# A feed-forward matrix as seven block products for eight, with its activations through DRAM

## The chip, the cores and the metric

The kernel is one program on one core of a Trainium2 chip. Its engines work side by side, each through its own list in order, and wait for each other by semaphores: TensorE (PE: matmuls; PEld: its weight loads), VectorE (DVE), ScalarE (ACT), GpSimd (POOL) and SyncE (SP), which issues nearly all DMAs. The metric is the device time of one execution in microseconds (us). Before the change it is 814.73 us, the median of three runs (813.27 to 820.41).

## The reference

One transformer block over 2048 positions of width 512: a normalised, modulated input goes through memory-augmented attention (32 heads of 16, four segments of 512 positions) and an output projection; the result is normalised again and goes through a feed-forward part of width 1792 with a GELU.

```python
h = _layernorm(x) * (1 + ca) + sa
x = x + ga * _A_ref(h, A_wq, A_wk, A_wv, A_wo, A_beta)   # attention, then o @ wo
h = _layernorm(x) * (1 + cb) + sb
x = x + gb * (_gelu(h @ w1 + b1) @ w2 + b2)
```

All is in float32. On TensorE the kernel writes each float32 factor as a high part (its cast to fp32r) and a low part (the rest), and a product as three matmuls: high by high, low by high, high by low.

## The kernel before, in words

Three stages follow each other, with overlaps. The first makes q, k, v and the memory terms. The second is attention: 64 steps, each for two heads of one segment, in an order that tables of numbers (`PRM`) write out by hand. A position in these tables is ten times the step plus a place in it. A step computes scores (L609) and their masked row maxima on VectorE (L616), the scores again transposed (L698) with exponentials on ScalarE (L713, L724), the causal masks on GpSimd (L701), and PV products (L738).

Four heads' PV output goes to DRAM and comes back regrouped; a *group* is eight heads of one segment, 16 in all, numbered U. VectorE takes the reciprocal of its row sums (L773), which goes to DRAM (`RD`) and is loaded back broadcast (`rbB`); the group is multiplied by it and the memory term is added (L787, L789; the *mix*), then it is cast and split (`oh`, `ol`). The memory term itself is first multiplied by a broadcast `rm` on GpSimd (L794). Groups 13 to 15 are mixed on VectorE, earlier ones on GpSimd. Four groups and the split `wo` make a segment's output projection: 48 matmuls (L815) in four blocks of positions `b`. Segments 0 to 2 do this during attention, in the one PSUM bank `mm`; segment 3 after it. The residual is added (L833) and the rows go to DRAM as `X2D`.

The third stage is the feed-forward part. A segment's rows are normalised (`ln2_*`), turned by four transposes for each of four blocks `d` of the width (L162), modulated on ScalarE and split. Segment 0's turns stand in attention, the other segments' in the feed-forward part. The first matrix has 14 output blocks of 128. For one block and one segment `ffn1_mm` issues 12 matmuls (four blocks `k` by three, L989) into one of three banks; ScalarE's GELU reads the bank (L992); VectorE casts and subtracts (L140, L141). All stays in SBUF. Four blocks later `ffn2` uses the result in 12 matmuls for the second matrix (L1073), into four banks `acc`. So the two matrices alternate: 12 matmuls of the first, 12 of the second, 56 times. The split weights of both stay in SBUF after the first segment.

Between attention and this alternation stands a transition: four blocks of the first matrix and the first half of segment 3's projection occupy TensorE while groups 14 and 15 come back from DRAM.

## Time and profile before

| | |
|---|---|
| median of three runs | 814.73 us (813.27 to 820.41) |
| the profiled execution, first to last instruction | 811.6 us |
| TensorE busy in it | 796.0 us |
| attention's last PV product ends at | 484.6 us |
| from there to the end | 327.0 us |
| matmuls 128x512 of the first / second feed-forward matrix | 672 / 672 |

The profiled execution's own time is its span; what lies around it in a run is part of the median's 3.1 us more. In a list of groups a line shows its place in the code, the engine, what is written from what, the count, the time busy, the mean of one in ns, and the engine's idle time before it with what ended that. In a list by time a line begins with the start and the duration in us; a bracket at its end names the wait before it. In a table of stretches each engine stands with its busy time and, in brackets, its instructions.

### The profile page before, as it was taken

The numbers are of one execution on the slowest core, as the hardware profiler recorded it, in microseconds if no ns is written. First come the engines' busy times: TensorE is split into PE (matmuls) and PEld (weight loads), VectorE is DVE, ScalarE is ACT, GpSimd is POOL, SyncE is SP. The second block draws the span as 40 slices with busy tenths as digits, with TensorE's granted clock in tenths as the row PEclk, the third lists the DMA queues.
The fourth block names the chain that finished last, engine by engine and source line by source line (L and its number), as shares of the span: only waits on it lengthen the run. The fifth ranks groups of instructions, "written<-read, shape, count | busy, mean of one in ns | idle before, by whom it ended". The sixth has DMA issues, their size and how long they took to land.

```text
span 811.6 us, 13638 instructions
## 1 busy us (share of the span) xinstructions
PE 796.0 (98%) x4669; PEld 546.9 (67%) x4669; DVE 502.7 (62%) x1373; ACT 368.5 (45%) x734; POOL 287.3 (35%) x508
## 2 busy tenths in 40 slices
PE   8999999999999999999999999999999999999998
PEld 4877777866444455445544548788888888888887
DVE  6686696469878877896687627874542353324223
...
GB/s 339 183 311 253 271 181 218 159 353 129 171 171 182 165 208 175 238 199 181 177 183 206 172 192 192 213 120 101 25 79 1 52 67 38 1 1 104 1 1 52
DMA packets 83566, 123.03 MB, mean 152 GB/s; under 512 B 14116, under 2 KB 46244, under 8 KB 82984
## 3 DMA queue, kind: packets, MB, share of 16 engines
...
q8 instruction: 36, 0.59, 0.3%
...
HBM read 75.60 MB, written 46.15 MB: 150 GB/s over the span
## 4 chain that ended last, share of the span: by engine, by line
PE 75%; DMA 8%; ACT 5%; DVE 4%; POOL 4%; issue 3%; SPq 1%; ACTq 0%; DVEq 0%; POOLq 0%
PE acc L1073 18%; PE f1b L989 16%; PE pv L738 6%; PE att L698 5%; PE q L330 5%; PE att L609 5%; PE k L330 4%; PE mm L815 3%; PE v L481 3%; DMA RD<-dn 2%; DMA rbB<-RD 2%; ACT pt L713 1%; PE nu L453 1%; DMA qst<-ms 1%; POOL pt L701 1%
## 5 line engine op out<-in xcount | busy, mean ns | idle before, releaser
L616 DVE CUSTOM_DVE_ANT_0 dump<-att,maskb 128x512 bf16<-128x512 f32 (+2 forms) x384 | 192.2, 553 | 27.2 <-PE att L609 24.3
L992 ACT ACTIVATE gt<-f1b,b1t 128x512 f32<-128x512 f32 x56 | 38.5, 688 | 245.8 <-PE f1b L989 195.0
L713 ACT ACTIVATE pt<-att 128x512 f32<-128x512 f32 (+1 forms) x256 | 126.1, 557 | 44.6 <-PE att L698 44.3
L701 POOL TENSOR_SCALAR_AFFINE_SELECT pt<-pt 128x256 f32<-128x256 f32 x256 | 100.1, 408 | 80.1 <-ACT pt L713 50.1
L140 DVE CAST gh<-gt 128x512 fp32r<-128x512 f32 x56 | 23.8, 425 | 163.0 <-ACT gt L992 163.0
L698 PE MATMUL att<-qst,kst 99*128 99x512 bf16 (+3 forms) x512 | 106.6, 300 | 5.5 <-ACT pt L724 2.1
L609 PE MATMUL att<-kst,qst 96*128 96x512 bf16 (+2 forms) x384 | 94.2, 326 | 0.7 <-DVE nm L616 0.2
L738 PE MATMUL pv<-pt,V 128*32 128x512 f32 (+2 forms) x992 | 88.3, 442 | 0.1
L1073 PE MATMUL acc<-w2h,gh 128*128 128x512 f32 (+1 forms) x224 | 86.7, 387 | 0.0
L1073 PE MATMUL acc<-w2l,gh 128*128 128x512 f32 (+1 forms) x224 | 86.0, 384 | 0.4 <-DVE w2l L141 0.4
L1073 PE MATMUL acc<-w2h,gl 128*128 128x512 f32 (+1 forms) x224 | 85.9, 383 | 0.0
L698 PEld LDWEIGHTS <-kst 99*128 99x128 bf16 x512 | 42.9, 97 | 56.9 <-issue 39.7
L989 PE MATMUL f1b<-hodd,w1h 128*128 128x512 f32 x224 | 73.7, 390 | 0.0
L724 ACT ACTIVATE pt<-att 128x512 f32<-128x512 f32 (+1 forms) x128 | 57.1, 512 | 22.9 <-PE att L609 19.9
L153 POOL TENSOR_SCALAR crs<-cmv 128x4 f32<-128x4 f32 x4 | 1.0, 247 | 170.8 <-DVE cmv L150 170.7
L609 PEld LDWEIGHTS <-qst 96*128 96x128 bf16 x384 | 33.2, 98 | 39.9 <-issue 24.6
L1073 PEld LDWEIGHTS acc<-w2l,gh 128*128 128x128 f32 x224 | 42.0, 188 | 9.1 <-DVE w2l L141 0.9
L989 PEld LDWEIGHTS f1b<-hodd,w1h 128*128 128x128 f32 x224 | 42.1, 188 | 8.6
L1073 PEld LDWEIGHTS acc<-w2h,gl 128*128 128x128 f32 x224 | 42.1, 188 | 8.4
L1073 PEld LDWEIGHTS acc<-w2h,gh 128*128 128x128 f32 x224 | 42.1, 188 | 8.3
L738 PEld LDWEIGHTS pv<-pt,V 128*32 128x32 f32 x992 | 22.2, 108 | 36.8 <-issue 26.2
L989 PE MATMUL f1b<-C0hh,w1l 128*128 128x512 f32 x112 | 43.7, 390 | 0.2 <-DVE w1l L141 0.2
...
## 6 DMA issues: line engine op xcount, KB each, us to landing
...
```

The costliest lines, as they stand in the source:

```text
L330: pe.matmul(ps, a[:, k, 128 * g:128 * g + 128], b[k], start=(k == 0 and i == 0), stop=(k == KB - 1 and i == 2))
L481: pe.matmul(ps, a[k][:, 128 * b:128 * b + 128], w[:, k, :], start=(k == 0 and i == 0), stop=(k == KB - 1 and i == 2))
L609: pe.matmul(ps, q_of(P, h, i), k_of(P, h, 128 * (i + 1)), start=True, stop=True)
L616: v.tensor_tensor_reduce(out=dump[n_dump[0] % 2][:, :n], in0=src, in1=maskb[:, 512 - n:], scale=-1.0, scalar=-4 * NEG, op0=ALU.add, op1=AL ...
L698: pe.matmul(ps, k[:99, e, 128 * j:128 * j + 128], q[:99, e, 128 * j:512], start=True, stop=True)
L701: pool.affine_select(out=t, in_=t, pattern=pattern, compare_op=ALU.is_ge, fill=0.0, base=0, channel_multiplier=-1)
L713: act.activation(pt[:, h, :], ps[:, :n], AF.Exp, scale=0.25)
L724: act.activation(pt, pv_, AF.Exp, scale=0.25)
L738: pe.matmul(ps[32 * c:32 * c + 32, lo:hi], V[4 * s + j][:, VW * hd:VW * hd + 32], pt[:, c % 2, lo - o:hi - o], start=start, stop=stop)
L989: pe.matmul(ps, a[:, k, :], b[k], start=(i == 0), stop=(i == 11))
L992: act.activation(g, ps, AF.Gelu_apprx_tanh, bias=b1t[:, f:f + 1])
L1073: pe.matmul((mm if lo else acc[b])[:, lo:hi], a[:, c], w[:, lo:hi], start=(f == 0 and i == 0), stop=(last and i == 2))
```

## The change

The first matrix is computed for two segments at once. Take output blocks f and f + 7 of the matrix, two segments a and b, and the two halves of the width over which the sum runs: a two-by-two product of blocks. Eight block products make it; Winograd's form of Strassen's method makes it from seven, with sums and differences of the blocks ahead and behind. Each block product here is six matmuls (two `k` by three). Seven of them are called a *quad*: 14 quads, seven for segments 0 and 1, seven for 2 and 3.

- Differences of the activations (`r_sub`, four times two operations on 128x512 for each pair of segments) and of the weights (`w_sub`, four operations on 128x256 for each quad) are made on GpSimd, then split: the high part on ScalarE, the low part on VectorE.
- In a quad ScalarE copies the bank X three times while products are still added to it, VectorE adds three times, and four GELUs follow. Their results go to DRAM (`GD`).
- The second matrix starts after the last quad. It loads the activations back from `GD`, three steps ahead, and splits them (`split_g`). It uses eight banks in turn by segment. Its weights are loaded, scaled on GpSimd and split during the last seven quads, into SBUF that the first pair's activations leave.
- Segment 1 is normalised and turned in attention as segment 0 is. Segment 2's output projection moves behind attention, ahead of segment 3's.

```diff
- 'wo': [[2, 10, 10, 10], [6, 10, 11, 11], [2, 10, 10, 11]],
+ 'wo': [[2, 10, 10, 10], [6, 10, 11, 11]],
- 'ht': 481,
- 'htd': 20,
- 'ln': [312, 339, 374, 408],
+ 'ht': [[465, 474, 481, 494], [614, 622, 629, 636]],
+ 'ln': [[312, 339, 374, 408], [498, 522, 566, 574]],
- 'wout': ['vvvv', 'vava', 'vava'],
+ 'wout': ['vvvv', 'vava', 'vvvv'],
- 'w1at': [58, 59, 60],
+ 'w1at': [58, 60],
...
+        def r_sub(p, n):
+            x, y = {"t1": ("b12", "b11"), "t2": ("b22", "b11"), "t3": ("b22", "b12"), "t4": ("b21", "b22")}[n]
+            for o, i, j in zip(hk(p, RAW[n]), hk(p, x), hk(p, y)):
+                pool.tensor_tensor(out=o, in0=i, in1=j, op=ALU.subtract)
...
+        def r_lo(p, n, k):
+            src = hk(p, RAW.get(n, n))[k]
+            v.tensor_tensor(out=R[p][n][1][k], in0=src, in1=R[p][n][0][k].bitcast(F32), op=ALU.subtract)
...
+            pool.tensor_tensor(out=b[:, i], in0=x, in1=y, op=ALU.add if i == 0 else ALU.subtract)
...
+        def prod(n, name, ps, start):
+            t, i = PW[name]
+            wh, wl = wt1[t][n % 2]
+            rh, rl = R[n // FH][name]
+            for k in range(2):
+                for c, (a, b) in enumerate(((wh, rh), (wl, rh), (wh, rl))):
+                    pe.matmul(ps, a[:, i, k, :], b[k], start=start and k == 0 and c == 0, stop=k == 1 and c == 2,
+                              skip_group_check=not start)
...
+            if not last:
+                prod(n, "b11", X, True)
+                act.activation(s1, X, AF.Copy)
+                step(0)
+                prod(n, "b21", Y, True)
+                add(s1, Y)
+                g_out(n, s1, s1, 0, 0)
+                step(1)
+            if not first:
+                prod(n - 1, "t4", bx[(n - 1) % 2], False)
+                g_out(n - 1, bx[(n - 1) % 2], s4, 1, 0)
+            step(2)
+            if not last:
+                prod(n, "t2", X, False)
+                act.activation(s2, X, AF.Copy)
+            step(3)
+            if not first:
+                o = st["2"][(n - 1) % 2]
+                prod(n - 1, "b22", bv[(n - 1) % 2], False)
+                add(o, bv[(n - 1) % 2])
+                g_out(n - 1, o, o, 0, 1)
+            step(4)
...
+            prod(n, "t1", V_, True)
+            step(5)
+            prod(n, "t3", X, False)
+            act.activation(s3, X, AF.Copy)
+            add(s3, V_)
+            g_out(n, s3, s3, 1, 1)
+            step(6)
...
+        for m in range(4):
+            bg(2 * FH - 1, 6, load_g, m)
+        for m in range(2):
+            bg(2 * FH, 2 + m, split_g, m)
...
+        for n, i, f, m in ((2, 3, r_split, "b11"), (3, 2, r_split, "b21"), (4, 0, r_sub, "t1"), (4, 1, r_split, "b22"),
+                           (4, 2, r_sub, "t3"), (4, 4, r_split, "t1"), (5, 0, r_sub, "t2"), (5, 1, r_split, "t3"),
+                           (5, 4, r_split, "t2"), (5, 5, r_sub, "t4"), (6, 1, r_split, "t4")):
+            bg(n, i, f, 1, m)
```

A *step* here is a place after a product, to which `bg` hangs other work: splits, sums and loads for later quads.

Three places of the instruction lists are spoken of below. The first is TensorE's list where attention ends; the first row is the last of the PV products. Before:

```order
L738 MATMUL att_2009<-pt_2_5897,V_153 32x256 x2
L989 MATMUL f1b_5946<-C0hh_0_4974,w1h_5987 128x512
L989 MATMUL f1b_5946<-C0hh_0_4974,w1l_5988 128x512
L989 MATMUL f1b_5946<-C0hl_0_4975,w1h_5987 128x512
L989 MATMUL f1b_5946<-C0hh_1_5095,w1h_5987 128x512
```

And now, where the 84 projection matmuls begin (L805 is `wo_part`), and where they go over into quad 0 (L1034 is `prod`):

```order
L728 MATMUL att_2065<-pt_2_5911,V_209 32x256 x2
L805 MATMUL mm<-woh,oh_4713 128x512
L805 MATMUL mm<-woh,ol_4715 128x512
L805 MATMUL mm<-wol,oh_4713 128x512
L805 MATMUL mm<-woh,oh_4975 128x512
```

```order
L805 MATMUL spare<-wol,oh_6099 128x512
L1034 MATMUL bx_5967<-r0b11h_5973,w1mh_6001 128x512
L1034 MATMUL bx_5967<-r0b11h_5973,w1ml_6002 128x512
L1034 MATMUL bx_5967<-r0b11l_5975,w1mh_6001 128x512
L1034 MATMUL bx_5967<-r0b11h_5974,w1mh_6001 128x512
```

The blocks of the first matrix that stood here have become projection work; the first product of quad 0 follows as the 85th matmul, and after its first three products (18 matmuls) stands the last part of segment 3's projection, which needs group 15.

The second place is VectorE's list in the transition. The mix of group 14 (L787 before, L777 now) stands ahead or behind; the rows are those between it and group 15's reciprocal. Before, with w1's splits ahead of the mix:

```order
L141 TENSOR_TENSOR w1l_5994<-w1r_5661,w1h_5993 128x512
L787 TENSOR_TENSOR opk_5851<-opk_5851,rbB_5933 128x512
L789 TENSOR_TENSOR opk_5851<-opk_5851,amB_5853 128x512
L804 TENSOR_TENSOR ol_6037<-opk_5851,oh_6035 128x512
L773 RECIPROCAL dn_6005<-dn_6005 128x32
```

And now (L995 is the low part of an activation block, L1024 of weights, L822 the residual's addition from PSUM):

```order
L777 TENSOR_TENSOR opk_5859<-opk_5859,rbB_5953 128x512
L779 TENSOR_TENSOR opk_5859<-opk_5859,amB_5861 128x512
L995 TENSOR_TENSOR r0b11l_5975<-hr_0_4931,r0b11h_5973 128x512
L794 TENSOR_TENSOR ol_6102<-opk_5859,oh_6099 128x512
L995 TENSOR_TENSOR r0b11l_5976<-hr_1_5008,r0b11h_5974 128x512
L1024 TENSOR_TENSOR w1ml_6002<-wa_5624,w1mh_6001 128x512
L1024 TENSOR_TENSOR w1ml_6002<-wb_6090,w1mh_6001 128x768
L995 TENSOR_TENSOR r0b21l_5979<-hr_2_5040,r0b21h_5977 128x512
L995 TENSOR_TENSOR r0b21l_5980<-hr_3_5130,r0b21h_5978 128x512
L822 TENSOR_TENSOR xb_0_5312<-mm,xb_0_5312 128x512
L763 RECIPROCAL dn_6086<-dn_6086 128x32
```

All splits of quad 0 now stand behind the mix of group 14; between the reciprocal and the mix of group 15 stand six more low parts of activations, two of weights and three more additions.

The third place is GpSimd's list after attention's last mask (L701). Before, it held two multiplications and then only the small normalisation steps of the later segments:

```order
L701 AFFINE_SELECT pt_3_5902<-pt_3_5902 128x256
L794 TENSOR_TENSOR amB_5853<-amB_5853,rm_5855 128x512
L794 TENSOR_TENSOR amB_6009<-amB_6009,rm_6011 128x512
L153 TENSOR_SCALAR crs_6240<-cmv_6239 128x4
L154 TENSOR_TENSOR crs_6240<-crs_6240,neg_half 128x4
```

Now, from the last of the first quad's four weight operations on, which stand behind group 14's multiplication (L784 is group 15's, L1009 `w_sub`, L984 `r_sub`):

```order
L1009 TENSOR_TENSOR wb_6090<-wa_5624,wb_6090 128x256
L984 TENSOR_TENSOR hr_0_4931<-hr_0_5814,hr_0_4931 128x512
L984 TENSOR_TENSOR hr_1_5008<-hr_1_5846,hr_1_5008 128x512
L784 TENSOR_TENSOR amB_6107<-amB_6107,rm_6109 128x512
L984 TENSOR_TENSOR hr_0_5814<-hr_2_5869,hr_0_5814 128x512
L984 TENSOR_TENSOR hr_1_5846<-hr_3_5927,hr_1_5846 128x512
L984 TENSOR_TENSOR hr_2_5869<-hr_2_5869,hr_0_4931 128x512
L984 TENSOR_TENSOR hr_3_5927<-hr_3_5927,hr_1_5008 128x512
L1009 TENSOR_TENSOR wb_6174<-wa_5747 128x256
```

Differences that overwrite their operand in place wait for the low part that still reads it. GpSimd's list goes on with four weight operations for each quad to the end of the first matrix.

434 lines of the change are left out of this document (244 added, 190 removed).

## The prediction

> **What bounds the kernel now.** I read the page first: the span, the busy shares, the granted clock and the chain that ended last.
>
> ```profile
> span 811.6 us, 13638 instructions
> PE 796.0 (98%) x4669; PEld 546.9 (67%) x4669; DVE 502.7 (62%) x1373; ACT 368.5 (45%) x734; POOL 287.3 (35%) x508
> ...
> PE 75%; DMA 8%; ACT 5%; DVE 4%; POOL 4%; issue 3%; SPq 1%; ACTq 0%; DVEq 0%; POOLq 0%
> PE acc L1073 18%; PE f1b L989 16%; PE pv L738 6%; PE att L698 5%; PE q L330 5%; PE att L609 5%; PE k L330 4%; PE mm L815 3%; PE v L481 3%; DMA RD<-dn 2%; DMA rbB<-RD 2%; ACT pt L713 1%; PE nu L453 1%; DMA qst<-ms 1%; POOL pt L701 1%
> ```
>
> TensorE carries 75% of the chain, and the two feed-forward products are its largest parts (18% and 16%). An average is not enough, so next come stretches: attention's last part, the whole feed-forward part, and fifty steady microseconds of it.
>
> ```profile
> core 0: us, PE busy (x) PEld busy (x) DVE busy (x) ACT busy (x) POOL busy (x), PEclk, DMA share, GB/s
> 200.00:484.60 284.60, 276.43 (x2242) 134.77 (x2241) 217.80 (x810) 204.88 (x464) 189.10 (x383) 1.00 0.64 185
> 484.60:811.60 327.00, 323.07 (x1483) 267.99 (x1482) 146.84 (x270) 56.91 (x86) 7.25 (x8) 1.00 0.21 67
> 640.00:690.00 50.00, 50.00 (x222) 41.42 (x221) 20.34 (x40) 6.58 (x10) 1.26 (x2) 1.00 0.13 43
> ```
>
> From 484.6 us on, TensorE is busy 323 of 327 us at clock 1.00, ScalarE 57, GpSimd 7. In the steady stretch 50 us hold 221 weight loads, one for each matmul: 0.226 us apiece. A row's own duration (0.39 us) is no price, since matmuls overlap; the distance of starts is. The waits of this part say the same:
>
> ```profile
> ACT gt L992 <- PE f1b L989: 195.0, 43, 5.1
> POOL crs L153 <- DVE cmv L150: 170.7, 3, 76.8
> DVE gh L140 <- ACT gt L992: 163.0, 49, 4.6
> ...
> PE f1b L989 <- DVE w1l L141: 0.2, 1, 0.2
> ```
>
> ScalarE waits 195 us in all for products, TensorE 0.2 us for split weights. A matmul removed here is worth its full distance, as long as the other engines still run ahead.
>
> **What is removed.** Before, two output blocks over two segments cost 4 x 12 = 48 matmuls; now a quad costs 7 x 6 = 42. Fourteen quads save 14 x 6 = 84 matmuls, 84 x 0.226 = **-19.0 us**. One quad lasts 42 x 0.226 = 9.5 us on TensorE. The transposes stay 64 in number, the output projection's matmuls too.
>
> **What is moved out of attention.** Segment 2's 48 projection matmuls (10.9 us) leave the last eight attention steps and stand after them; segment 1's four turns come in. On TensorE that adds to nothing. The rows for the stretch that they leave:
>
> ```profile
> 375.00:400.00 25.00, 24.63 (x187) 13.75 (x186) 17.36 (x65) 15.34 (x36) 20.48 (x35) 1.00 0.58 169
> ...
> 450.00:475.00 25.00, 25.00 (x193) 13.48 (x189) 10.84 (x42) 17.30 (x41) 15.80 (x32) 1.00 0.60 174
> ...
> L157 POOL TENSOR_SCALAR xt<-xt,cmv,crs 128x512 f32<-128x512 f32 x4 | 8.3, 2071 | 0.0
> ...
> 482.26 2.35 PE L738 MATMUL att<-pt,V 128*32 128x512 f32 x28 [1.84 <-POOL pt L701]
> ```
>
> GpSimd, at 15.8 of 25 us, gets four normalisations of 2.07 us there in less time; it masks what PV waits for. Loss up to 3.7 us (8.3 us of new work against 9.2 us of idle time, of which a stretch shorter by 10.9 us leaves perhaps half); gain up to 1.84 us, if the quoted stall goes. The nearest row is the same work for segment 0, at 372 to 393 us: GpSimd was at 20.5 of 25 us there, and TensorE still at 24.6. So I take 0.
>
> **The transition.** Call the end of attention's last PV product E, now 484.6 us. Behind it TensorE has 84 projection matmuls and three products of quad 0 (18), then the part that needs the last pair group's output: 102 x 0.226 = 23.1 us of cover. VectorE's side starts from the mix of group 14, whose broadcast load lands 4.0 us after its issue at 486.83, so at E + 6.2.
>
> ```profile
> 482.51 4.30 DMA RD<-dn
> 486.81 0.02 issue
> 486.83 0.59 SPq L782
> ...
> 496.52 4.00 DMA rbB<-RD
> ...
> 506.75 2.49 DVE xb L833 x4
> ```
>
> From there to the last low part of the attention output, VectorE's list holds 17 operations on 512 columns with both inputs in SBUF, three on 1280 columns in all (2.5 more), four additions from PSUM, and a reciprocal with its scaling (0.6 us). At 0.62 us each (2.49 for four) that is 12.1 + 2.5 + 0.6 = 15.2 us: E + 21.4, 1.7 us ahead of TensorE. Alone, it fits.
>
> But GpSimd now works beside it: seven operations on 512 columns and four on 256.
>
> ```profile
> L787 POOL TENSOR_TENSOR opk<-opk,rbB 128x512 f32<-128x512 f32 x13 | 16.5, 1271 | 6.8 <-DMA rbB<-RD 4.0 <-DMA TD<-ts 2.8
> L672 POOL TENSOR_TENSOR nm<-nm 128x16 f32<-128x16 f32 x64 | 14.1, 220 | 15.0 <-DVE nm L620 12.5
> ...
> 494.90 1.59 POOL L794 TENSOR_TENSOR amB<-amB,rm 128x512 f32<-128x512 f32 x1 [7.47 <-DMA rm<-rdd]
> 494.93 0.42 DVE L140 CAST gh<-gt 128x512 fp32r<-128x512 f32 x1
> 495.38 1.67 DVE L141 TENSOR_TENSOR gl<-gt,gh 128x512 fp32r<-128x512 f32 x1
> ...
> 497.42 0.69 DVE L141 TENSOR_TENSOR gl<-gt,gh 128x512 fp32r<-128x512 f32 x1
> ...
> 465.48 1.28 POOL L804 TENSOR_TENSOR ol<-opk,oh 128x512 fp32r<-128x512 f32 x1
> 466.31 0.69 DVE L833 TENSOR_TENSOR xb<-mm,xb 128x512 f32<-128x512 f32 x1 [1.83 <-PE mm L815]
> ```
>
> The same subtraction took 1.67 us beside a GpSimd operation and 0.69 us without: 0.98 of 1.27 us lost, and GpSimd itself went from 1.27 to 1.59. An addition that reads PSUM kept its 0.69. A GpSimd operation on 256 columns isn't in the trace; between 1.27 (512) and 0.22 (16) I estimate 0.75. So GpSimd has 7 x 1.27 + 4 x 0.75 = 11.9 us in this stretch, of which 3.1 can lie beside the additions and the reciprocal. If the other 8.8 excludes VectorE, the list ends at E + 30.2, 7.1 us behind TensorE, and some 2 us more before quad 1 (third and fourth differences, next weights). Bounds 0 to 9; the nearest row lost three quarters of an operation, so I take three quarters of 8: **+6**.
>
> [...]
>
> **The quads that prepare the second pair** (4 and 5). Both together last 19.0 us on TensorE. With two SBUF inputs VectorE has the weights' low parts, 1792 columns a quad or 3.5 operations on 512, and eight low parts of activations: 15 x 0.62 = 9.3 us; GpSimd eight differences (10.2) and eight weight sums (6.0): 25.5 us, if they exclude each other, 6.5 too many. That backlog reaches TensorE only through VectorE's additions, and nothing of the second pair is read until quad 7, so quad 6 takes part of it up. Bounds 0 to 6.5, and I take **+2**. In the last seven quads VectorE adds two low parts of the second matrix and GpSimd two scalings: 3.4 + 5.5 = 8.9 of 9.5 us, so 0 where the two alternate well, and up to 0.7 a quad (one GpSimd operation that falls badly), which I leave to the rivals.
>
> **The start of the second matrix.** Before, its first products were hidden in the first one. Now the first activations come back from DRAM, and their load stands on SP's queue behind quad 13's last store, in a buffer that staged the second matrix.
>
> ```profile
> L992 ACT ACTIVATE gt<-f1b,b1t 128x512 f32<-128x512 f32 x56 | 38.5, 688 | 245.8 <-PE f1b L989 195.0 <-issue 43.6 <-DVE opk L789 7.1
> L138 ACT ACTIVATE w2h<-w2r 128x512 fp32r<-128x512 f32 x14 | 8.8, 626 | 3.1 <-DVE w2r L1010 2.9
> L132 ACT ACTIVATE ts<-att 128x512 f32<-128x512 f32 x1 | 0.6, 597 | 1.8 <-PE att L738 1.8
> ...
> 509.63 6.97 DMA xt<-X2D
> ```
>
> After the last product of quad 13: copy 0.60, addition 0.62, GELU 0.69, store issued 0.3, a 256 KB load between 1.7 us (a quarter of the 1 MB load's 6.97) and 4.0 (the broadcast), cast 0.63, subtraction 0.69: 5.2 to 7.5 us. Two products (12 matmuls) cover 2.7. Bounds +2.5 to +4.8; I take the middle, **+3.5**. Stores and loads of 14.7 MB each way lie beside 140 us and more of matmuls where the DMA share was 0.13: nothing.
>
> **Sum.** -19.0 + 0 + 6 + 2 + 3.5 = -7.5 us. The profiled execution would go from 811.6 to 804.1; the median stands 3.1 us over that span, so I forecast 814.7 - 7.5 = **807.2 us**.
>
> **Rivals.**
> - *The cover holds.* Transition 0, pair 0, attention's stall gone (-1.8), second matrix +2.5: -18.3, 796.4 us. For it: without exclusion VectorE ends 1.7 us ahead, and the last seven quads leave ScalarE idle. Against it: the 1.67 row. 0.20.
> - *The exclusion takes its full price.* 9 + 6.5 + 4.8, and 0.3, half of that 0.7, in each of the last seven quads (2): 22.3 - 19.0 = +3.3, 818.0 us, no difference or a hair slower. For it: the 1.67 and 1.59 rows; against it, the slack between a difference and its use. 0.19. [...]
> - *Slower: the quad is bound by ScalarE behind VectorE.* The product t2 is added into the bank that ScalarE has just copied out. Between b11's end and t2's start lie 12 matmuls, 2.7 us; the copy takes 0.60 and stands on ScalarE's queue behind the previous quad's last GELU (0.69), which waits for VectorE's addition. From the point where that addition comes more than about 1.4 us late, TensorE waits in every quad. ScalarE has 3 x 0.60 + 4 x 0.69 + 3.5 x 0.63 = 6.8 us a quad, 8.0 with two casts of the second matrix, so a quad of 11.5 us is what two exposed queues would make: 14 x 2.0 = 28; -19 + 28 + 3.5 = +12.5, 827 us. Against it: 1.5 us of idle ScalarE a quad, two sets of banks. 0.13.
>
> That fewer matmuls are not what is run can be left out: the instruction lists show 588 for 672.
>
> **How the numbers follow.** Forecast 0.48, with its own range 803 to 812. 1%, 8.1 us, is about what a measurement of this kernel can tell from no change. Below 806.6 lie the first rival (0.20) and the lower 0.43 of the forecast (0.21): faster 0.41. Above 822.9 lies the slower rival with a little of the second: 0.14. The rest, 0.45, is within 1%. The range 796 to 819 leaves out most of the slower rival and the low half of the first.
>
> **What would show it.** Right: steady quads of 9.5 us; gaps of 5 to 8 us on TensorE at the t2 product and the last projection part, ended by VectorE operations of 1.3 to 1.7 us; one gap of 3 to 4 us ahead of the first product of the second matrix, ended by a low part that waited for a load. Wrong: no subtraction over 0.7 us in the transition (the first rival), or gaps at t2 in each quad ended by ScalarE's copy (the last).

## The result, and the profile after

The changed kernel takes 869.24 us (median of four, 868.23 to 872.19) against 816.23 for the kernel before on the same chip: a ratio of 1.0654, with a 95% interval of 1.0611 to 1.0696. The forecast was 807.2 us, its range 796 to 819. It is slower, 42 us above even the slower rival's 827.

The page of the profiled execution: the span, the engines' busy time, and the chain that ended last by engine and by line.

```profile
span 866.3 us, 14158 instructions
PE 807.9 (93%) x4585; PEld 544.0 (63%) x4585; DVE 545.8 (63%) x1370; ACT 466.8 (54%) x914; POOL 384.5 (44%) x593
...
PE 60%; DVE 9%; issue 9%; DMA 9%; ACT 7%; POOL 5%; SPq 0%; ACTq 0%; DVEq 0%; POOLq 0%
```

TensorE has 84 matmuls fewer (4585 for 4669) and yet 12 us more busy time. Its share of the chain falls from 75% to 60%. The stretches say where: attention's last part, the feed-forward part, fifty microseconds of quads, and two stretches inside attention.

```profile
200.00:487.92 287.92, 273.16 (x2210) 128.92 (x2209) 216.01 (x808) 206.76 (x466) 191.79 (x384) 0.98 0.62 182
487.92:866.30 378.38, 338.61 (x1430) 271.27 (x1430) 192.21 (x269) 153.15 (x264) 102.08 (x93) 0.94 0.45 146
640.00:690.00 50.00, 42.02 (x150) 31.88 (x149) 27.32 (x33) 27.73 (x50) 23.03 (x21) 0.86 0.47 153
...
375.00:400.00 25.00, 24.64 (x199) 13.07 (x199) 17.87 (x68) 16.27 (x38) 21.56 (x33) 1.00 0.53 162
450.00:475.00 25.00, 20.89 (x163) 8.13 (x164) 13.70 (x52) 15.79 (x36) 22.36 (x34) 0.95 0.66 179
```

In the steady stretch 149 weight loads stand where there were 221, and the granted clock is 0.86 where it was 1.00. At 450 to 475 us TensorE is busy 20.9 of 25 us (it was 25.0) and GpSimd 22.4 (15.8).

Four stretches carry the account: attention, quads 0 and 1, quads 2 to 7, quads 8 to 12. The quads are read from the starts of their b11 products. The forecast's column is its own sum laid over the same stretches.

| us | forecast's sum | measured | more |
|---|---|---|---|
| attention's last PV product ends (E) | 476.1 | 487.9 | 11.8 |
| E to quad 0 | 19.0 | 19.4 | 0.4 |
| quads 0 and 1 | 26.8 | 38.8 | 12.0 |
| quads 2 to 7 | 62.1 | 74.6 | 12.5 |
| quads 8 to 12 | 47.5 | 69.9 | 22.4 |
| quad 13 to the second matrix | 15.7 | 16.3 | 0.6 |
| second matrix | 156.9 | 159.4 | 2.5 |
| span | 804.1 | 866.3 | 62.2 |

(E by the forecast is 484.6, less the 10.9 us that leave attention, and 2.4 more for segment 1's four turns, which come in. A quad is 42 x 0.226 = 9.5 us; quad 0 has 30 of these matmuls, since t4 and b22 of each quad lie in the next; the last stretch has 54 and the 3.5 us of the second matrix's start. The second matrix is what is left of 804.1; the 2.5 us more are its first segment's, which took 40.3 us where the others took 38.1. Group 15's twelve projection matmuls, 2.7 us, and the 32 transposes of segments 2 and 3, 0.6 us for four, lie in quads 0 to 7.)

Who waits for whom, from E to the end (in all, times, longest):

```profile
ACT s L1039 <- DVE s L1043: 63.3, 42, 5.0
...
POOL hr L1204 <- DMA hr<-in_w: 49.7, 7, 8.8
POOL wb L1009 <- DMA wa<-in_w: 43.1, 6, 12.3
PEld bx L1034 <- ACT s L1056: 30.0, 10, 6.9
...
ACT gh L135 <- DMA hr<-GD: 3.7, 2, 2.8
...
PEld bx L1256 <- ACT gh L135: 3.3, 1, 3.3
```

Ten times in the 14 quads the first weight load of t2 waits for L1056, ScalarE's copy of X: 30.0 us. This is the row that the prediction named as the sign of its third rival, which had it in each quad. What holds ScalarE is seen in one turn of the loop that quads 9 to 12 repeat every 13.7 to 14.0 us. First SyncE's queue, then GpSimd, ScalarE, VectorE and TensorE:

```profile
642.85 0.97 SPq L1201 DMA_DIRECT2D hr<-in_w  x2
...
647.98 1.30 POOL L1204 TENSOR_TENSOR hr<-hr,gab 128x512 f32<-128x512 f32 x1 [7.39 <-DMA hr<-in_w]
649.23 0.74 POOL L1009 TENSOR_TENSOR wb<-wa 128x256 f32<-128x256 f32 x1
649.93 1.28 POOL L1204 TENSOR_TENSOR hr<-hr,gab 128x512 f32<-128x512 f32 x1
...
649.30 0.63 ACT L135 ACTIVATE r0t2h<-hr 128x512 fp32r<-128x512 f32 x1 [1.02 <-POOL hr L1204]
649.84 0.40 ACT L1020 ACTIVATE w1th<-wa 128x256 fp32r<-128x256 f32 x1
651.25 0.63 ACT L135 ACTIVATE r0t2h<-hr 128x512 fp32r<-128x512 f32 x1 [1.00 <-POOL hr L1204]
651.78 0.58 ACT L1081 ACTIVATE s<-bx 128x512 f32<-128x512 f32 x1
654.42 0.72 ACT L1039 ACTIVATE s<-s,b1t 128x512 f32<-128x512 f32 x1 [2.06 <-DVE s L1043]
655.04 0.40 ACT L1020 ACTIVATE w1th<-wb 128x256 fp32r<-128x256 f32 x1
655.35 0.58 ACT L1056 ACTIVATE s<-bx 128x512 f32<-128x512 f32 x1
...
649.97 1.79 DVE L138 TENSOR_TENSOR r0t2l<-hr,r0t2h 128x512 fp32r<-128x512 f32 x1 [2.45 <-ACT r0t2h L135]
...
652.56 1.22 DVE L138 TENSOR_TENSOR r0t2l<-hr,r0t2h 128x512 fp32r<-128x512 f32 x1
653.70 0.68 DVE L1043 TENSOR_TENSOR s<-bv,s 128x512 f32<-128x512 f32 x1
...
655.98 0.50 PE L1034 MATMUL bx<-r1t2h,w1mh 128*128 128x512 f32 x1 [1.91 <-ACT s L1056]
```

Two row blocks of the second matrix are loaded behind the last quad's stores and land 5.1 us after their issue. GpSimd scales them, the second behind a weight sum, until 651.2. ScalarE's queue holds their two casts (L135; they write into `r0t2`, which the first pair has left) **ahead of** t3's copy (L1081). T3's last matmul started at 649.15; its copy starts at 651.78 and ends at 652.36. VectorE's queue adds to this: the two low parts (L138) stand ahead of the addition that needs the copy, and it starts at 653.70, 1.3 us behind the copy's end. GELU and the next quad's copy of X follow late, and t2 waits until 655.98. The next quad's loads are issued behind the stores that came late, and so the loop is closed.

### The profile page after: what moved, and what is told of

Its sections match the earlier page's. It is cut to its first block, busy times and chain, and to the rows that moved or that the text cites. A ratio compares the mean times of both kernels' runs of the same rounds, so it can differ in the third digit from the quotient of the medians.

```text
span 866.3 us, 14158 instructions
## 1 busy us (share of the span) xinstructions
PE 807.9 (93%) x4585; PEld 544.0 (63%) x4585; DVE 545.8 (63%) x1370; ACT 466.8 (54%) x914; POOL 384.5 (44%) x593
## 4 chain that ended last, share of the span: by engine, by line
PE 60%; DVE 9%; issue 9%; DMA 9%; ACT 7%; POOL 5%; SPq 0%; ACTq 0%; DVEq 0%; POOLq 0%
PE pv L728 7%; PE att L688 6%; PE bx L1256 5%; PE q L315 5%; PE att L599 5%; PE by L1256 4%; PE bv L1256 4%; PE k L315 4%; PE mm L805 3%; PE v L466 3%; POOL wb L1009 2%; PE spare L1256 2%; PE bx L1034 2%; DMA qst<-ms 2%; PE mm L1256 2%
## 5 line engine op out<-in xcount | busy, mean ns | idle before, releaser
L138 DVE TENSOR_TENSOR gl<-hr,gh 128x512 fp32r<-128x512 f32 x56 | 38.8, 692 | 100.2 <-ACT gh L135 100.2
L135 ACT ACTIVATE gh<-hr 128x512 fp32r<-128x512 f32 x56 | 35.4, 632 | 113.9 <-PE spare L1256 56.3
L714 ACT ACTIVATE pt<-att 128x512 f32<-128x512 f32 (+1 forms) x128 | 56.9, 508 | 21.9 <-PE att L599 19.9
L1039 ACT ACTIVATE s<-s,b1t 128x512 f32<-128x512 f32 x42 | 30.4, 723 | 63.3 <-DVE s L1043 63.3
L599 PEld LDWEIGHTS <-qst 96*128 96x128 bf16 x384 | 33.3, 98 | 40.3 <-issue 25.0
L1009 POOL TENSOR_TENSOR wb<-wa 128x256 f32<-128x256 f32 x28 | 26.8, 956 | 44.3 <-DMA wa<-in_w 43.1
L728 PEld LDWEIGHTS pv<-pt,V 128*32 128x32 f32 x992 | 22.5, 109 | 37.8 <-issue 27.1
L610 DVE TENSOR_REDUCE nm<-att 128x2 f32<-128x256 f32 x64 | 27.2, 425 | 23.1 <-PE att L646 19.1
L1204 POOL TENSOR_TENSOR hr<-hr,gab 128x512 f32<-128x512 f32 x14 | 18.7, 1344 | 49.7 <-DMA hr<-in_w 49.7
L606 DVE DVE_READ_ACCUMULATOR2_ANT nm<- 128x1 f32 x384 | 32.0, 83 | 0.0
L511 POOL TENSOR_TENSOR q<-qr,q 128x512 bf16<-128x512 f32 x16 | 18.7, 1168 | 27.5 <-ACT q L510 27.1
L502 POOL TENSOR_SCALAR qp<-qp 128x512 f32<-128x512 f32 x12 | 18.8, 1563 | 26.1 <-ACT qp L497 26.1
L1043 DVE TENSOR_TENSOR s<-bv,s 128x512 f32<-128x512 f32 x28 | 19.1, 682 | 16.2 <-PE bv L1034 11.1
L984 POOL TENSOR_TENSOR hr<-hr,hr 128x512 f32<-128x512 f32 x16 | 24.1, 1522 | 9.3 <-DVE r0b11l L995 6.0
L315 PE MATMUL q<-Ahl,wqh 128*128 128x512 f32 x64 | 25.8, 404 | 0.1
```

Source lines behind the costliest of these rows:

```text
L135: act.activation(hi, src, AF.Copy)
L138: lo_eng.tensor_tensor(out=lo, in0=src, in1=hi.bitcast(F32), op=ALU.subtract)
L315: pe.matmul(ps, a[:, k, 128 * g:128 * g + 128], b[k], start=(k == 0 and i == 0), stop=(k == KB - 1 and i == 2))
L599: pe.matmul(ps, q_of(P, h, i), k_of(P, h, 128 * (i + 1)), start=True, stop=True)
L606: v.tensor_tensor_reduce(out=dump[n_dump[0] % 2][:, :n], in0=src, in1=maskb[:, 512 - n:], scale=-1.0, scalar=-4 * NEG, op0=ALU.add, op1=AL ...
L714: act.activation(pt, pv_, AF.Exp, scale=0.25)
```

## The experiments

The table has each run's ratio to the kernel before on the same chip, and from its profile the end of attention (E) and the lengths of the same stretches.

| run | ratio (95%) | E | E to q0 | q0-1 | q2-7 | q8-12 | q13 on | span |
|---|---|---|---|---|---|---|---|---|
| the changed kernel | 1.0654 (1.0611-1.0696) | 487.9 | 19.4 | 38.8 | 74.6 | 69.9 | 16.3 | 866.3 |
| w2_early | 1.0489 (1.0460-1.0517) | 488.2 | 19.1 | 39.7 | 74.6 | 53.4 | 16.6 | 850.2 |
| cast_late | 1.0456 (1.0417-1.0495) | 489.0 | 19.7 | 41.2 | 73.8 | 51.3 | 17.4 | 851.3 |
| gelu_late | 1.0629 (1.0586-1.0671) | 490.4 | 19.1 | 38.8 | 71.6 | 66.4 | 17.6 | 863.2 |
| fill_t2 | 1.0684 (1.0640-1.0728) | 485.8 | 19.1 | 39.7 | 76.1 | 66.4 | 18.8 | 865.3 |
| no_sub | 1.0459 (1.0396-1.0522) | 491.9 | 19.8 | 36.9 | 68.0 | 59.3 | 17.6 | 853.5 |
| v_sums | 1.0624 (1.0556-1.0692) | 490.7 | 19.2 | 40.0 | 75.5 | 63.3 | 18.6 | 866.6 |
| no_apply1 | 1.0665 (1.0618-1.0711) | 483.5 | 19.1 | 39.7 | 74.8 | 69.5 | 16.4 | 862.3 |
| apply_v | 1.0630 (1.0582-1.0677) | 484.8 | 19.7 | 40.1 | 74.8 | 69.6 | 16.7 | 865.0 |
| den_early | 1.0684 (1.0646-1.0723) | 490.7 | 19.1 | 38.2 | 73.7 | 68.6 | 18.7 | 868.7 |
| trans | 1.0621 (1.0546-1.0696) | 488.1 | 23.8 | 32.4 | 74.7 | 68.6 | 18.4 | 866.5 |
| ln_later | 1.0589 (1.0528-1.0651) | 486.2 | 19.1 | 31.5 | 74.8 | 67.9 | 17.1 | 856.1 |
| comb1 | 1.0273 (1.0227-1.0319) | 487.5 | 19.1 | 28.9 | 73.6 | 50.6 | 16.5 | 836.4 |
| comb2 | 1.0228 (1.0164-1.0291) | 485.1 | 23.6 | 23.7 | 73.2 | 48.3 | 16.3 | 829.4 |
| comb3 | 1.0300 (1.0245-1.0355) | 488.4 | 24.0 | 26.0 | 71.8 | 55.3 | 16.4 | 841.0 |
| comb4 | 1.0282 (1.0237-1.0327) | 488.1 | 19.9 | 27.1 | 82.6 | 47.6 | 13.4 | 836.6 |
| comb5 | 1.0231 (1.0194-1.0267) | 486.6 | 20.4 | 25.8 | 80.9 | 48.8 | 13.4 | 833.8 |
| comb6 | 1.0094 (1.0069-1.0119) | 488.3 | 19.1 | 25.4 | 71.8 | 49.5 | 13.4 | 825.3 |
| comb7 | 1.0053 (1.0025-1.0080) | 488.0 | 19.1 | 21.8 | 70.6 | 51.0 | 13.4 | 822.0 |

E differs by up to 7 us among runs whose attention is the same (485.1 to 491.9), so spans alone are no measure of one edit; the stretches are.

### Quads 8 to 12: a load, or a place in a queue?

w2_early:

```diff
-                bg(n, 0, load_w2, f)
+                bg(n - 1, 0, load_w2, f)
```

> The loads of the second matrix's rows are issued one quad earlier; nothing else is changed. Queue theory (in quads 8 to 12 the copy of t3's bank stands on ScalarE's queue behind a cast that waits for GpSimd's scaling of a row block loaded 5 us earlier, so that the whole quad waits for a transfer): quads 8 to 12 fall from 13.7 us to 10 to 11.5 us each, TensorE's wait at t2 of 2.30 us goes, and the kernel's time falls from 869 to 846 to 856 us. Exclusion theory (the quads are long because VectorE runs slowly beside GpSimd): the same operations stand beside one another, the quads stay at 13.7 us, and the time stays within 3 us of 869.

These quads fall from 14.0 to 10.7 us each, 16.5 us in all, and hardly anything else moves. But the edit changes two things: the data come earlier, and so the casts wait less. cast_late keeps the late load and moves the split, that is the two casts on ScalarE's queue and the two low parts on VectorE's:

```diff
-                bg(n, 4 + i, split_w2, f)
+                bg(n, 6, split_w2, f)
```

> The two splits of the second matrix's rows go from before t1 and t3 to the quad's end, behind t3's copy and the addition and GELU of s3; loads and scalings stay where they are. If the place on ScalarE's queue counts (the cast waits, and t3's copy stands behind it), quads 8 to 12 fall from 13.7 to 10.5 to 12 us and the time from 869 to 853 to 861 us. If the late transfer itself counts, the wait moves to the next quad's copy, these quads keep 13 us or more, and the time stays within 4 us of 869.

ScalarE's list in that run, and in w2_early; the casts are L135, t3's copy L1081, the copy of X L1056:

```profile
645.21 0.60 ACT L1081 ACTIVATE s<-bx 128x512 f32<-128x512 f32 x1 [0.79 <-ACT w1th L1020]
...
647.50 1.14 ACT L135 ACTIVATE r0t2h<-hr 128x512 fp32r<-128x512 f32 x2
648.54 0.58 ACT L1056 ACTIVATE s<-bx 128x512 f32<-128x512 f32 x1
```

```profile
643.03 0.63 ACT L135 ACTIVATE r0t2h<-hr 128x512 fp32r<-128x512 f32 x1 [0.77 <-POOL hr L1204]
643.57 0.58 ACT L1081 ACTIVATE s<-bx 128x512 f32<-128x512 f32 x1
```

With the transfer as late as before and the split behind t3's copy and addition the quads take 10.3 us, less than with the early load (10.7). VectorE's part is seen too: in cast_late the copy ends at 645.81 and the addition starts at 645.84; in w2_early, whose low parts keep their place, the copy ends at 644.15 and the addition starts at 645.50. So two things make the wait together: data that come late, and a **place ahead of t3's copy and its addition on two queues**, ScalarE's and VectorE's. Undoing either one takes most of the wait away. How much each of the two queues counts was not tested by a run of its own.

gelu_late takes the third rival at its word, by which the copy of X waits behind the last GELU:

```diff
                 act.activation(s1, X, AF.Copy)
+                if not first:
+                    g_out(n - 1, s3, s3, 1, 1)
...
-            g_out(n, s3, s3, 1, 1)
+            if n == 2 * FH - 1:
+                g_out(n, s3, s3, 1, 1)
```

> The last GELU of a quad (that of s3) is put on ScalarE's queue behind the next quad's copy of X into s1, and no longer ahead of it. Third rival of the prediction, taken literally (the copy waits behind that GELU, which waits for VectorE's addition): TensorE's wait at t2 goes in the quads from 1 on, each falls by 2 to 4 us, and the time is 830 to 845 us. Queue theory with the second matrix's staging as the holder: the wait of 2.30 us at t2 in quads 8 to 12 goes or shrinks, but t3's copy still stands behind the cast, so these quads keep 12 to 13.7 us and the time is 850 to 865 us. Exclusion theory: no change beyond 3 us.

In quads 8 to 12 TensorE's wait at t2 goes, and a wait of 1.5 to 3.9 us at t4 takes its place:

```profile
638.06 0.50 PE L1034 MATMUL bx<-r1t4h,w1th 128*128 128x512 f32 x1 [3.68 <-ACT s L1083]
```

L1083 is t3's copy in that run, still behind the cast. Quads 8 to 12 gain 3.5 us of 22. The chain that the rival named is there (addition 653.70, GELU 654.42, copy 655.35 above), but what makes it late in these quads stands ahead of t3's copy.

### The clock

Inside the loop of the changed kernel the clock falls. The stretches are 3.41 us long, laid on the times at which it changes (TensorE busy, weight loads, VectorE, ScalarE, GpSimd, then the clock):

```profile
622.50:625.92 3.42, 2.38 (x11) 1.61 (x9) 3.42 (x3) 1.11 (x2) 3.42 (x4) 1.00 0.00 0
625.92:629.33 3.41, 1.50 (x7) 0.96 (x6) 2.26 (x5) 2.46 (x5) 0.67 (x1) 1.00 0.28 87
629.33:632.74 3.41, 3.41 (x10) 2.63 (x9) 1.09 (x2) 2.09 (x4) 0.00 (x0) 0.50 1.03 298
632.74:636.16 3.42, 3.42 (x16) 2.81 (x16) 0.69 (x1) 1.38 (x3) 1.98 (x3) 1.00 0.60 228
```

A window with TensorE busy 1.50 of 3.41 us is followed by one at half clock, in which 10 matmuls start and not 16. fill_t2 puts work in the place of the wait:

```diff
             if not last:
+                if not first:
+                    for _ in range(10):
+                        pe.matmul(spare, R[0]["b11"][0][0][:, :128], R[0]["b11"][0][0], start=True, stop=True)
                 prod(n, "t2", X, False)
```

> In quads 1 to 13 ten matmuls of 128x128 by 512 into an idle bank, which nobody reads, stand on TensorE between t4 and t2 of the quad: 2.3 us of work in the place of the wait. Clock theory (the wait itself lowers the granted clock to 0.5 for 3.4 us behind it, and this costs 1.7 us each time): the clock stays at 1.00 through quads 8 to 12. If the slow matmuls are on the path, each quad is 1.7 us shorter and the time is 845 to 855 us; if the period of these quads is set by other engines (queue theory), they keep 13.7 us at a clock of 1.00 and the time is within 6 us of 869. If the low clock has another cause than the wait, it is still seen, and the time is 869 or up to 30 us more for the added matmuls.

From 620 to 665 us, the changed kernel and then this run:

```profile
620.00:665.00 45.00, 37.73 (x139) 28.70 (x139) 24.70 (x28) 22.99 (x42) 22.55 (x22) 0.89 0.47 153
```

```profile
620.00:665.00 45.00, 41.17 (x178) 32.76 (x177) 27.00 (x31) 24.05 (x43) 24.05 (x24) 1.00 0.45 147
```

The clock stays at 1.00 there, so the drops follow from the waits. Yet quads 8 to 12 still take 13.3 us each (14.0): other engines set their length there, and TensorE's half rate lies in its own slack. In quads 2 to 7 the added work costs as much as the clock brings (76.1 for 74.6), so what it costs there stays open.

### VectorE beside GpSimd

no_sub leaves the sums out, v_sums gives them to VectorE:

```diff
-            x = (wb if src else wa)[j][:, o:o + hi - lo]
+            x = (wb if src and j < 2 else wa)[j][:, o:o + hi - lo]
...
-                for i in range(4):
-                    bg(n, 3 + i, w_sub, n + 2, i)
...
-        for n, i, f, m in (..., (4, 0, r_sub, "t1"), ..., (4, 2, r_sub, "t3"), ..., (5, 0, r_sub, "t2"), ..., (5, 5, r_sub, "t4"), ...):
```

> GpSimd's sums and differences in the quads are left out: the weight sums from quad 2's weights on (the raw blocks are split in their place) and the second pair's activation differences, so that the products from quad 2 on are of wrong operands; VectorE, ScalarE and TensorE run the same list, and GpSimd keeps the second matrix's scalings and the normalisation's small operations. Exclusion theory (VectorE's low parts run at up to twice their time beside GpSimd, its additions come late, and so the GELU and the copy that t2 waits for): quads 5 and 6 fall from 14.3 and 13.4 to 9.5 to 10.5 us, and the time from 869 to 853 to 861 us. Queue theory: quads 8 to 12 keep 13 us or more here, since the late load, its scaling and the cast are still there; if the exclusion makes those too, they fall to 10.5 us or less, and the time to 840 to 848 us.

```diff
-            pool.tensor_tensor(out=b[:, i], in0=x, in1=y, ...)
+            (pool if j < 2 else v).tensor_tensor(out=b[:, i], in0=x, in1=y, ...)
...
-                    bg(n, 3 + i, w_sub, n + 2, i)
+                    bg(n, 5 + i // 2, w_sub, n + 2, i)
...
-                pool.tensor_tensor(out=o, in0=i, in1=j, op=ALU.subtract)
+                (v if p else pool).tensor_tensor(out=o, in0=i, in1=j, op=ALU.subtract)
```

> The weight sums of the quads (two steps later) and the second pair's activation differences are made by VectorE and no longer by GpSimd. Exclusion theory (the two engines lengthen each other's operations, and quads 5 and 6 are late by that): VectorE's low parts keep 0.6 to 0.7 us for 512 columns, quads 5 and 6 fall from 14.3 and 13.4 to 9.5 to 11 us, quads 8 to 12 from 13.7 to 11.5 to 13 us, and the time from 869 to 850 to 860 us, though VectorE has more to do. If the load of VectorE counts and not the exclusion, these quads are as long as before or longer, and the time is 869 to 885 us.

The low parts of t1 in the second pair, grouped (busy us, mean ns): the changed kernel, then v_sums.

```profile
L995 DVE TENSOR_TENSOR r1t1l<-hr,r1t1h 128x512 fp32r<-128x512 f32 x2 | 2.9, 1476 | 1.3 <-ACT r1t1h L989 1.3
```

```profile
L995 DVE TENSOR_TENSOR r1t1l<-hr,r1t1h 128x512 fp32r<-128x512 f32 x2 | 1.3, 688 | 1.3 <-ACT r1t1h L989 1.3
```

The slowing beside GpSimd is real: 1476 ns for one in the changed kernel, where two of GpSimd's differences run beside them (2.98 us from 584.57), and 688 in v_sums. Yet with the sums on VectorE quads 5 and 6 take 13.7 and 14.0 us (14.3 and 13.4 before). Without the sums they take 10.3 and 10.6. So the added work makes them long, and taking the slowing away by giving this work to VectorE brings nothing: a longer list there costs as much. The path is seen in the changed kernel's quad 5: the two low parts of t1 (2.9 us) stand ahead of an addition (588.36), the GELU (589.07) and the copy of X (590.01) come behind it, and t2 waits 2.4 us.

Quads 8 to 12 fall to 11.9 us without the sums, below the 13 that the queue theory had set. Both queues have a share in this: GpSimd's second scaling follows the first at once there, and with shorter low parts the addition starts 0.3 us behind t3's copy and no longer 1.3.

### Attention

no_apply1 and apply_v, each alone:

```diff
-                ap(ln[3] + PRM["lnd"][1] * b, ln2_apply, i, b, pool)
+                if i == 0:
+                    ap(ln[3] + PRM["lnd"][1] * b, ln2_apply, i, b, pool)
```

> The four normalisations of segment 1's rows, which GpSimd makes in the last part of attention (4 by 2.07 us), are left out; segment 1 then goes into the feed-forward part unnormalised. If GpSimd bounds the last part of attention there, its last product comes 6 to 9 us earlier (at 479 to 482 us in place of 487.5) and the time is 858 to 864 us. If the product moves by less than 2 us, the loss in attention has another cause (segment 1's turns, or the drops of the clock), and the time stays within 3 us of 869.

```diff
-                ap(ln[3] + PRM["lnd"][1] * b, ln2_apply, i, b, pool)
+                ap(ln[3] + PRM["lnd"][1] * b, ln2_apply, i, b, v if i else pool)
```

> Segment 1's four normalisations in attention are made by VectorE and not by GpSimd, nothing else is changed. If GpSimd is the bound of attention's last part, its last product comes at 479 to 481 us (it came at 481 to 488 in the runs so far with an unchanged attention, at 479.1 where they were left out), and the time falls by 2 to 5 us; if VectorE's masks are then late instead, the product comes at 484 or later.

Without the normalisations E comes 4.4 us earlier, with them on VectorE 3.1. (The second text counts by the start of the last product into the bank pv: 483.5 in the changed kernel, 479.1 and 480.4 in these.) Neither is far outside what E varies by, and neither time differs from the changed kernel's.

The kept traces show the share more clearly. ScalarE has the same 384 exponentials of attention in every run, so each can be laid beside its like in the kernel before. From the 361st to the 371st (466.5 and 473.5 us there) the lag grows by 3.9 to 5.2 us in all 14 runs in which GpSimd makes segment 1's normalisations, and by 0.5 in the five in which it doesn't. So they cost about 4 us at that place. Another 2.4 us of the changed kernel's lag stand already at the 271st (395.0 us), up to which runs with the same list differ by -1.3 to +5.6 us from the kernel before. Some 5 us are left open: between 400 and 485 us the trace has TensorE waiting for a row maximum on GpSimd (3.2 us), loads of those maxima (2.2 us) and turns (1.2 us), and two drops of the clock (to 0.5, for 3.41 us each, at 431.4 and 472.3).

### Ahead of quad 0, and quads 0 to 3

In the changed kernel quad 0's t2 waits 6.8 us for the copy of X, and ScalarE's rows say behind what: group 15's cast.

```profile
515.99 0.63 ACT L129 ACTIVATE oh<-opk 128x512 fp32r<-128x512 f32 x1 [4.39 <-DVE opk L779]
516.52 0.58 ACT L1056 ACTIVATE s<-bx 128x512 f32<-128x512 f32 x1
```

den_early issues that group's chain sooner:

```diff
         r_lo(0, "b11", 1)
+        rest(15, "den", "rb_in")
         r_sub(0, "t1")
...
         wo_x(3, 0)
-        rest(15, "den", "rb_in")
...
         wo_x(3, 2)
+        rest(15, "mix", "o_hi", "o_lo")
...
-        rest(15, "mix", "o_hi", "o_lo")
```

> Group 15's reciprocal, its store to DRAM and its broadcast load are issued right behind group 14's mix and no longer behind segment 2's first sum, store and reload on VectorE's and SyncE's queues; its mix and its split follow segment 2's third sum. Nothing else is changed. Transition theory (TensorE's wait of 6.8 us at quad 0's t2 is the copy of X standing on ScalarE's queue behind group 15's cast, and that cast waits for a store and a load which SyncE issued late): quad 0 falls from 18.2 to 10 to 12 us, and the time from 869 to 859 to 864 us. Exclusion theory (VectorE's list is too long there whatever the order): quad 0 keeps 16 us or more, and the time stays within 3 us of 869.

It brings nothing (17.9 us for 18.2), as the exclusion theory had set, but the trace names another holder: the memory rows' load slipped behind it, GpSimd's queue stood still for them with t3's and t2's differences behind, and the copy of X now stood behind the casts of t2.

```profile
510.63 1.29 POOL L784 TENSOR_TENSOR amB<-amB,rm 128x512 f32<-128x512 f32 x1 [8.68 <-DMA rm<-rdd]
511.88 6.03 POOL L984 TENSOR_TENSOR hr<-hr,hr 128x512 f32<-128x512 f32 x4
```

trans rewrites the whole stretch:

```diff
+        rest(15, "am_in", "den", "rb_in")
...
+        r_split(0, "b22")
+        r_sub(0, "t3")
+        r_sub(0, "t2")
...
+        r_split(0, "t2")
...
-        wo_x(3, 0)
...
+        for b in range(4):
+            wo_x(3, b)
...
-        rest(15, "mix", "o_hi", "o_lo")
...
+        bg(0, 0, rest, 15, "mix", "o_hi", "o_lo")
```

> Only the stretch between attention and quad 0 is rewritten: group 15's loads and its reciprocal first, segment 2's four sums and stores ahead of all four reloads of x (they alternated, so that each reload waited on SyncE's queue for its store), the splits that t2 needs ahead of t1's, and group 15's mix and casts behind the copy of X into s1. Queue theory for quad 0 (the 6.8 us at t2 are the copy of X behind group 15's cast on ScalarE, and the splits of t2 behind a long list): quad 0 falls from 18.2 to 10.5 to 13 us, the load of segment 2's rows is issued 5 us or more earlier, so that quad 1's waits shrink too (20.6 to 14 to 18 us), and the time goes from 869 to 855 to 862 us. If VectorE's and GpSimd's lists are too long there in any order (exclusion theory), quad 0 keeps 15 us or more and the time stays at 864 or above.

Quad 0 falls to 13.0 us, but 4.9 us of waiting now stand ahead of its first product. That product writes a bank that VectorE has to read out first, and this addition had come late. The sum of both stretches changes by 0.8 us. In neither run has VectorE a pause of 1 us between 493.6 us and group 15's mix, so another order there only chooses what comes late; comb6 below shortens the list by using the 8.6 us in which VectorE waited before.

ln_later moves the normalisations of segments 2 and 3. In the changed kernel quad 1's addition stood behind statistics that waited for a load, and behind that addition the GELU and the copy of X:

```profile
528.90 0.69 DVE L146 BATCH_NORM_STATS2 cst<-xt 128x6 f32<-128x512 f32 x1 [1.91 <-DMA xt<-X2D]
...
530.52 0.66 DVE L1043 TENSOR_TENSOR s<-bv,s 128x512 f32<-128x512 f32 x1
...
531.21 0.72 ACT L1039 ACTIVATE s<-s,b1t 128x512 f32<-128x512 f32 x1 [4.95 <-DVE s L1043]
```

```diff
-        for s, (n, i) in ((2, (0, 5)), (3, (2, 4))):
+        for s, (n, i) in ((2, (1, 0)), (3, (3, 3))):
...
-            at_(4, ln2_applies, s)
+            at_(4, ln2_applies, s, (0, 1))
+            at_(5, ln2_applies, s, (2, 3))
...
-                at_(6 + d, ln2_turn, s, d)
+                at_(8 + d, ln2_turn, s, d)
```

> The normalisations of segments 2 and 3 start two and six steps later in the quads, the four applications of each are put into two steps, the turns two steps further behind them, and the second pair's differences and splits later to suit. Load theory (VectorE's statistics wait for a 1 MB load and hold the addition of s3 behind them, and TensorE's turns wait for the applications): the waits at quad 1's and quad 3's t2 (3.5 and 2.7 us) and at quad 1's transposes (5 us) go, quads 1 and 3 fall from 20.6 and 16.1 to 11 to 13 us each, and the time from 869 to 856 to 861 us. If these quads are long for another reason (ScalarE's and VectorE's load there), they keep 15 us or more and the time stays within 4 us of 869.

Quads 0 and 1 lose 7.3 us; quads 2 to 7 keep theirs, since quad 2 now has the turns and 15.7 us. The intervals of the two ratios overlap, so the gain is shown by the trace alone.

### All together

comb1 joins w2_early, gelu_late, den_early and ln_later; comb2 has trans in place of den_early, and the second matrix's scalings one quad earlier; comb3 is comb2 with v_sums.

```diff
-                bg(n, 2 + i, scale_w2, f)
+                bg(n - 1, 5 + i, scale_w2, f)
```

> Four edits together: the second matrix's rows loaded one quad earlier (16 us alone), the last GELU behind the next quad's copy (4 us alone), group 15's chain early, the normalisations of segments 2 and 3 later. If the waits have separate causes, the gains add up: 869 - 16 - 4 - 6 - 10 = 833, so 828 to 838 us, with quads 8 to 12 at 9.5 to 10.3 us. If they hide one another (an engine that is late in one place would be late in the next anyway), the time stays above 842 us. The exclusion theory alone would leave quads 5 and 6 at 11 us or more.

> The rewritten stretch ahead of quad 0, the second matrix's rows loaded and scaled one quad earlier, the last GELU behind the next quad's copy, and the normalisations of segments 2 and 3 later, all together; the sums stay on GpSimd. Without the stretch and with the scaling in its old quad these edits gave 837 us. Queue theory: quad 0 and quad 1 fall by 6 to 8 us in all and the waits at t4 of quads 8 to 12 (1 us each) go: 822 to 830 us. Exclusion theory: quads 4 to 6 keep 13 us.

> The run before this one with the sums and differences of the quads on VectorE, GpSimd keeping the scalings. Exclusion theory: quads 4 to 6 fall to 9.5 to 11 us and the time to 808 to 820 us, the same as the kernel before within 1%. If VectorE's longer list makes its additions late instead, the quads are 10.5 to 12 us throughout and the time is 825 to 840 us.

comb1 gains 31 us by the ratios, where its four parts alone add up to 18; by the profiled spans it is 29.9 against 27.0. With intervals of about 0.4% on each ratio this shows that the gains add up, and not that the causes hid each other. comb2 (836.2 us) missed its 822 to 830, mostly in quads 2, 4 and 6 (16.7, 12.3 and 14.0 us). But in it quads 8 to 12 take 9.7 us each, so the steady rate of the forecast can be had. With the sums on VectorE (comb3) they take 11.1. The sums stand in its list ahead of the additions there, and t3 waits about 1 us in each quad for ScalarE's second copy.

comb4 puts the first splits ahead of group 14's mix, spreads the second pair's work in single steps, and loads the second matrix's first activations early into idle buffers; comb5 adds apply_v.

```diff
+        def gt_(m):
+            return hrt[5 + m] if m < 3 else hrt[m % 4]
...
-            bg(2 * FH - 1, 6, load_g, m)
+            bg(2 * FH - (1 if m == 3 else 2), 6, load_g, m)
```

> All edits of comb2, and besides: the first splits of quad 0 ahead of group 14's mix, where VectorE was idle for 8 us; the normalisations, turns, differences and splits of the second pair in single steps of quads 0 to 6; the first three activations of the second matrix loaded one quad earlier into idle buffers. If each wait had its own cause in the order of work, the 4.7 us ahead of quad 0, the excess of quads 0, 2, 4 and 6 (3.5 + 7 + 3 + 4.5 us) and most of the 3.2 us ahead of the second matrix go: 806 to 816 us, that is the forecast's steady quads and the time of the kernel before or a little less. If the engines' sums are the bound in quads 0 to 6 (exclusion theory), these quads keep 12 us or more on the mean and the time is 818 to 830 us.

> The run before this one, and segment 1's normalisations on VectorE. 2 to 5 us less than it: 802 to 813 us.

Both miss their forecasts by more than 20 us (839.5 and 834.3 us). The early activation loads take away the whole wait at the second matrix (16.3 to 13.4 us). The first splits take away most of the wait ahead of quad 0 (23.6 to 19.9 us), but quad 0 grows from 13.0 to 16.5. The single steps are a miss: quads 2 to 7 grow by 9 us, with waits for the normalisations at quad 4's turns and for ScalarE's copies in quad 6.

comb6 has the sums that stand ahead of quad 0, and the second pair's differences, on VectorE; the turns two steps apart. In it two loads of the second matrix come too early: one overwrites an operand of the second pair's t2 before the difference is formed, the other t4 before its split, so that both are of other numbers there and t4's cast waits 2.9 us for its load. Its quads 1 and 7 take 14.5 and 18.1 us, with two new waits among others: ScalarE's copy of X for a store behind a late load (5.7 us), and that of t4's cast. comb7 puts these loads later, and quad 0's last weight splits back.

```diff
-            pool.tensor_tensor(out=b[:, i], in0=x, in1=y, ...)
+            (pool if j else v).tensor_tensor(out=b[:, i], in0=x, in1=y, ...)
...
-                pool.tensor_tensor(out=o, in0=i, in1=j, op=ALU.subtract)
+                (pool if (p, n) == (0, "t4") else v).tensor_tensor(out=o, in0=i, in1=j, op=ALU.subtract)
```

> All edits of comb2 and the earlier activation loads of comb4; besides, ahead of quad 0 the weight sums, three of the four differences and the first splits are made by VectorE while it waited, group 15's reciprocal stands right behind group 14's mix, and t1's and t3's splits come behind the addition of s1; the turns of segments 2 and 3 stand two steps apart, and the second pair's differences are VectorE's; segment 1's normalisations are VectorE's. Order theory (each wait has its place in the order of work): no wait of 2 us or more ahead of quad 0 and at its last projection part, quads 8 to 13 at 9.5 us, the sum of quads 0 to 7 at 88 to 94 us (comb2: 97), time 808 to 820 us. If VectorE's list is the bound there, the sum of quads 0 to 7 is 97 us or more and the time 825 us or more.

```diff
-            bg(n - 1, 0, load_w2, f)
+            bg(n - 1, 3 if j < 2 else 0, load_w2, f)
```

> The run before this one with the last two weight splits of quad 0 back ahead of it, and the first four row blocks of the second matrix loaded in the middle of quads 6 and 7. Order theory: quad 1 falls from 14.5 to 10 to 11.5 us, quad 7 from 18.1 to 10 to 11.5 us, nothing else changes, and the time falls from 825 to 811 to 816 us: the same as the kernel before within 1%, and above the forecast of 807 by what is left in the quads with turns and in attention. If the waits move on again, quads 2 to 8 take them up and the time stays at 820 us or above.

```profile
span 822.0 us, 14149 instructions
PE 786.3 (96%) x4585; PEld 532.4 (65%) x4585; DVE 545.9 (66%) x1392; ACT 464.2 (56%) x914; POOL 353.1 (43%) x571
...
488.04:507.16 19.12, 19.12 (x85) 15.81 (x85) 15.93 (x26) 7.46 (x14) 3.65 (x2) 1.00 0.33 112
507.16:663.94 156.78, 146.18 (x633) 115.52 (x631) 114.82 (x169) 108.26 (x195) 75.85 (x74) 0.99 0.59 193
```

Ahead of quad 0 TensorE is busy 19.12 of 19.12 us, in the quads 146 of 157 at a clock of 0.99. TensorE and ScalarE run as many instructions as in the changed kernel; 22 went from GpSimd to VectorE. Quad 1 came to 10.5 us as expected, quad 7, at 15.8, missed its 10 to 11.5, and quads 8 and 9 take 11.2 each (10.6 and 9.5 in comb6): in part the waits moved on, as the second branch has it. The time is 821.34 us, not the 811 to 816 expected, and 1.0053 of the kernel before: the same within 1%, and still not faster. No run beat the kernel before.

## Why the prediction was wrong

- **The matmuls.** 84 fewer were run, and at a clock of 1.00 their distance is 0.227 us. As TensorE's work the -19.0 held.
- **Attention, 0 us (bounds -1.84 to +3.7).** Wrong. It took for granted that TensorE's 8.5 us less (10.9 of projection out, 2.4 of turns in) would show as an earlier E. E came 3.3 us later. Of these 11.8 us GpSimd's normalisations are about 4, the price that the prediction had as its upper bound; 2.4 stood there before the first changed row of the list. The rest isn't settled.
- **The transition, +6 (0 to 9).** The gap at t2 was foreseen in place and size (5 to 8 us; 6.8), in part by luck. VectorE's list is as late as the exclusion's full price had it: its last low part of the attention output ends at E + 29.7 (30.2), with single operations of 1.5 to 1.8 us. But that was to end the gap itself. What t2 waits for is the copy of X, on ScalarE's queue behind group 15's cast, and at the last projection part no gap is left. What was missed is quad 1, where statistics waited for a load with the addition behind them. Quad 0 took 2.7 us and quad 1 9.3 us more than a sum that has the 6 in it.
- **The quads of the second pair, +2 (0 to 6.5).** 12.5 us more over quads 2 to 7, some 7 of them in quads 5 and 6. The prediction had the backlog reach TensorE through VectorE's additions, but counted on slack up to quad 7; it reached the copy of X in the same quad, through addition and GELU. The rest is in quads 2 and 3, beside segment 3's normalisation, for which the sum has no term.
- **The other quads, 0 (up to 0.7 each).** This is the step that failed most: 22.4 us in five quads. It compared sums (8.9 us of VectorE and GpSimd in 9.5) and set loads and stores at nothing. It didn't ask which events of other engines ScalarE's and VectorE's queues wait for ahead of the copies and additions that TensorE needs. cast_late shows it: the same work in another place brings 18.6 us back.
- **The second matrix, +3.5.** 2.85 us of waiting at its first product, inside the bounds, and behind it a stretch at half clock (0.5 for 3.41 us from 707.8, in which the matmuls start 0.43 us apart and not 0.227): its first segment took 40.3 us, in comb4 38.7. comb4 shows that early loads take away all of the wait.
- **The rivals.** The third one's mechanism was right in sign and place: t2 waits for ScalarE's copy of X. It was priced at 28 us by a quad of 11.5 us, for which it gives no sum, and had 0.13 because ScalarE has 1.5 us to spare. A queue that waits for others needs no full engine: ScalarE is busy 27.7 of 50 us in the steady stretch above, and the quads last 13.7. The slowing that the second rival rests on was seen (1476 against 688 ns above), but in the quads taking it away by v_sums brings no time; the rival's 818.0 was for a schedule with no other waits.

comb7 shows what is left. Its quads and the second matrix's start take 156.8 us; by the forecast's sum they were to take 152.1. What it has left over the forecast's span of 804.1 is 17.9 us, and 11.9 of these are attention's.
